# An attention and gated-MLP kernel: GpSimd's products and differences go to VectorE, and the first chunk's second product becomes native fp32

## The chip, the cores and the metric

The kernel runs on one core of one Trainium2 chip. The metric is device time in microseconds (us). Before the change three runs gave 677.52, 677.85 and 678.15 us, so the median is 677.85.

The core has a matrix engine (TensorE, PE), whose weight loads are listed apart (PEld), and four others: VectorE (DVE), ScalarE (ACT), GpSimd (POOL) and SyncE (SP), which here issues nearly all transfers. Each engine executes its own instructions in the order in which they were written, and waits on semaphores for the others.

## What is computed

Attention over 4 batches of 8 heads, 768 positions and 64 dimensions, followed by an MLP on the 3072 x 512 result. Cut to what matters:

```python
k_sum = k.reshape(B, H, nb, block, D).max(axis=3)      # block = 32, nb = 24
v_sum = v.reshape(B, H, nb, block, D).mean(axis=3)
scores_l = scale * q @ k.T        # kept where |i - j| < 16
scores_s = scale * q @ k_sum.T + log(32)
a = softmax(concat(scores_l, scores_s))
x = a @ concat(v, v_sum)          # heads side by side: 3072 x 512
h = x @ w_in                      # 512 x 2048
g = h * erf(softplus(h))
out = g @ w_out                   # 2048 x 512
```

The two weight matrices come as float64, the rest as float32.

## The kernel before

**Chunks and periods.** The 3072 tokens are worked on in 8 chunks of 384. The hidden dimension of 2048 is cut into 4 groups of 512, so that there are 32 periods (k = 0 to 31); period k belongs to chunk k // 4 and group k % 4. A period does the first product of its group (`mm1`, lines 499-511), reads it out of PSUM (`hout`: tanh on ScalarE, a copy on VectorE), applies ln and erf on ScalarE (`logs`, `erfs`), and runs the second product of the period before (`mm2`, lines 555-567), which accumulates over the four groups of a chunk in three PSUM banks. In between stands the attention of a quad, one pair of heads of a chunk, four to five periods ahead: `scores`, `softmax`, `transp`, `av`, `xsplit`. The four quads of the first chunk are done before period 0, interleaved with its `mm1`.

**Precision.** A float32 number is cut into a high and a low part in the format fp32r, and a product becomes three matmuls: high by high, high by low and low by high. `xsplit` makes the parts of x (xh, xl), `gsplit` those of g (gh, gl), `convert` those of the weights. Each weight unit is 128 x 2 x 512 numbers, 16 units in all, eight of w_in and eight of w_out, two for each group.

**Converting a weight unit** (lines 259-285) takes five instructions: three on VectorE (lines 266, 269, 272) assemble a float32 word out of the raw halves of a float64 by shifts and masks, ScalarE casts it into the high part (line 276), and GpSimd subtracts to get the low part (line 279). All 16 are converted once, between the first quads and period 3, so that within the first chunk every product uses parts.

**GpSimd's share.** Beside those 16 subtractions, GpSimd makes the product g = wt x h (line 543) in the first periods (`k < early`, which is 5), where ScalarE casts the high part of g and xsplit's high part, and VectorE makes the low part (line 550). From period 5 on all of `gsplit` and `xsplit` is VectorE's. GpSimd also copies the block summaries into the key window (line 371) and, for the first chunk, into the value window (line 355).

**Buffers.** Sixteen SBUF slots of one unit each (w0 to w15) hold the weights. A raw unit lands in its slot and the parts are written over it. Before that some slots hold the first chunk's keys, queries, probabilities and values (line 310). The last two, w14 and w15, serve as scratch for the float32 words (`homes`, line 248), so the last two units of w_out are loaded only in period 3 (line 666).

**The order of the work.** The operations are first collected with their reads and writes (class `Plan`, lines 45-159). `Plan.due` gives each operation a due time, counted back from the matmuls that need it; `Plan.order` then fills the engines one instruction at a time by estimated durations, taking the ready operation that is due first, and where an operation may run on two engines, the one that would end it first. TensorE's operations stay nearly in written order, with a window of 60 operations for the first 330. SP issues the transfers in planned order too: one that waits for a buffer holds up those behind it. In the gaps of the first stretch `busy` (line 595) writes filler matmuls on zeros.

Of the kernel before, what the change touches and what calls it, by code (L numbers as in the profile page):

```python
# [9 lines left out]
F32 = mybir.dt.float32  # L10
# [13 lines left out]
T = S // NTH  # L24
# [16 lines left out]
def f32(ap):  # L41
    return ap.bitcast(F32)
# [120 lines left out]
def block_attention_mlp(ctx: ExitStack, tc: tile.TileContext, q_t, k_nat, k_win, v_tok, v_nat, v_win, w_in, w_out, out):  # L163
# [61 lines left out]
    slot_of = {u: n for n, u in enumerate(units)}  # L225
    tiles, raws, whl = {}, {}, {}

    def slot(n, shape, dtype, name):
        return sb(shape, dtype, name, f"w{n}")

    def wname(u):
        n = slot_of[u]
        return [f"w{n}"] + ([f"w{n}a", f"w{n}b"] if n in (14, 15) else [])

    def load_w(u):
        kind, g, r = u

        def go():
            rw = raws[u] = slot(slot_of[u], [128, 2, 512, 2], U32, "rw")
# [5 lines left out]
        dma(1049, go, w=wname(u))  # L245


    homes = ["w14a", "w14b", "w15a", "w15b"]
    part_of = {}

    def temp(home):
        if home[0] == "t":
            return sb([128, 2, 512], F32, "a32", home)
        n = home[1:3]
        if n not in part_of:
            part_of[n] = slot(int(n), [128, 2, 2, 512], F32, "a32s")
        return part_of[n][:, "ab".index(home[3])]

    def convert(u, home):

        w, s = wname(u), {}

        def a():
            s["t"] = temp(home)
            s["a"], s["rw"] = s["t"].bitcast(U32), raws.pop(u)
            nc.vector.tensor_scalar(s["a"], s["rw"][..., 1], 3, 0x3FFFFFFF, op0=ALU.logical_shift_left, op1=ALU.bitwise_and)  # L266

        def b():
            nc.vector.scalar_tensor_tensor(s["a"], s["rw"][..., 0], 29, s["a"], op0=ALU.logical_shift_right, op1=ALU.bitwise_or)  # L269

        def c():
            nc.vector.scalar_tensor_tensor(s["a"], s["rw"][..., 1], 0xC0000000, s["a"], op0=ALU.bitwise_and, op1=ALU.bitwise_or)  # L272

        def high():
            whl[u] = slot(slot_of[u], [128, 2, 2, 512], F32R, "w")
            nc.scalar.copy(whl[u][:, 0], s["t"])  # L276

        def low(e):
            e.tensor_tensor(whl[u][:, 1], s["t"], f32(whl[u][:, 0]), op=ALU.subtract)  # L279
# [30 lines left out]
    V_SLOTS, K_SLOTS, Q_SLOT, P_SLOTS, W_SLOTS = (14, 15), (7, 8), 9, (10, 11), (12, 13)  # L310
# [188 lines left out]
    def mm1(k, f, ccs=range(4)):  # L499
        ch, g = divmod(k, NG)  # L500
        bank = hbank(k, f)

        def go(cc):
            if cc == 0:
                hs[k, f] = tiles[bank] = ps(bank, bank)
            w = whl["i", g, cc // 2][:, :, cc % 2, f * 128:(f + 1) * 128]
            for n, (m, x) in enumerate(((0, 0), (0, 1), (1, 0))):
                nc.tensor.matmul(hs[k, f][:, 0:T], lhsT=w[:, m], rhs=xt[ch, cc][x], start=(cc == 0 and n == 0), stop=(cc == 3 and n == 2))  # L508
        for cc in ccs:
            n = (ch * NP + cc) % NX  # L510
            pe(0.52, lambda cc=cc: go(cc), wname(("i", g, cc // 2)) + [f"xh{n}", f"xl{n}"], [bank])

    def hout(k, f):
# [24 lines left out]

    def gsplit(k, n, mult, cast, sub):
        s = (2 * k + n) % 3  # L540

        def mul(e):
            e.tensor_tensor(hc[k, n], wt.pop((k, n)), hc[k, n], op=ALU.mult)  # L543

        def high(e):
            gs[k, n] = [sb([128, 2, T], F32R, m, f"{m}{n}") for m in ("gh", "gl")]
            copy(e, gs[k, n][0], hc[k, n])

        def low(e):
            e.tensor_tensor(gs[k, n][1], hc.pop((k, n)), f32(gs[k, n][0]), op=ALU.subtract)  # L550
        on(mult, mul, [f"wt{s}"], [f"hc{s}"])
        on(cast, high, [f"hc{s}"], [f"gh{n}"])
        on(sub, low, [f"hc{s}", f"gh{n}"], [f"gl{n}"])

    def mm2(k, fs=range(G), ts=range(NT)):
        ch, g = divmod(k, NG)

        def go(i, t):
            if g == 0 and i == 0:
                os_[ch, t] = tiles[f"o{t}"] = ps("ops", f"o{t}")  # L560
            x, w = gs[k, i // 2], whl["o", g, i // 2][:, :, i % 2]
            for n, (m, y) in enumerate(((0, 0), (0, 1), (1, 0))):
                nc.tensor.matmul(os_[ch, t], lhsT=x[y][:, i % 2, t * 128:(t + 1) * 128], rhs=w[:, m],  # L563
                                 start=(g == 0 and i == 0 and n == 0), stop=(g == NG - 1 and i == G - 1 and n == 2))
# [62 lines left out]
    for names_, slots in ((["kf0", "kf1"], K_SLOTS[:1]), (["kf2", "kf3"], K_SLOTS[1:]), (["qf0", "qf1", "qf2", "qf3"], (Q_SLOT,)),
                          (["pr0", "pr1"], P_SLOTS[:1]), (["pr2", "pr3"], P_SLOTS[1:]), (["vwf0", "vwf1", "vwg0", "vwg1"], W_SLOTS[:1]),
                          (["vwf2", "vwf3", "vwg2", "vwg3"], W_SLOTS[1:]), (["vt0"], V_SLOTS[:1]), (["vt1"], V_SLOTS[1:])):
        for n in slots:  # L630
            for m in [f"w{n}"] + ([f"w{n}a", f"w{n}b"] if n in V_SLOTS else []):
                P.last[m] = [y for x in names_ for y in P.last[x]]
                P.readers[m] = [y for x in names_ for y in P.readers.get(x, [])]
# [92 lines left out]
    import json; json.dump([[o['n'],o['on'],o['start'],o['end'],o['due'],o['r'],o['w'],sorted(o['deps'])] for o in plan],open('/tmp/plan.json','w'),default=list)  # L726
# [47 lines left out]
```

## Time and profile before

| | |
|---|---|
| median of 3 runs | 677.85 us |
| profiled execution, its own time | 678.82 us |
| span of the profiled execution | 677.0 us |
| TensorE busy | 654.4 us (97%) |
| VectorE busy | 432.5 us (64%) |
| ScalarE busy | 475.1 us (70%) |
| GpSimd busy | 82.7 us (12%) |
| mean granted TensorE clock | 0.989 |
| moved by DMA | 64.52 MB |

Rows of the profile name a line, an engine, an operation, the tiles written and read, the shape, and how many. In tables by group there follow the busy time, the mean of one in ns, and the engine's idle time before them with what ended it. In a timeline the first two numbers are the start and the length in us; instructions that follow each other are merged, and the records of neighbours overlap by somewhat under 0.1 us. Matmuls are pipelined, so that the length of one matmul's record is longer than the distance to the next. A native fp32 matmul shows as two records.

### The profile page before, as it was taken

The page shows a single profiled execution, that of the slowest core. Times are in us where ns is not written, and L with a number is a line of the kernel's source. Part 1 is how long each engine was busy: PE and PEld are TensorE (multiplying, and loading weights), DVE is VectorE, ACT ScalarE, POOL GpSimd, SP SyncE. Part 2 cuts the span into 40 slices and gives each one's busy share as a digit, 9 for nine tenths or more (in the row PEclk, how much of TensorE's full clock was granted, in tenths as well). Part 3 has the DMA queues.
Part 4 walks back from the last instruction along what each step waited for, and adds up shares of the span by engine and source line. Part 5 has one row for each costly group of instructions (what it writes and reads, how often), then busy time and mean ns, then how long its engine had stood idle before and what let it go on. Part 6 is the DMA issues. An engine that isn't in the chain of part 4 may idle for free.

```text
span 677.0 us, 11588 instructions
## 1 busy us (share of the span) xinstructions
PE 654.4 (97%) x4646; PEld 567.9 (84%) x4653; DVE 432.5 (64%) x637; ACT 475.1 (70%) x869; POOL 82.7 (12%) x75
## 2 busy tenths in 40 slices
PE   9889689989999999999999999999999999999997
PEld 4667478879988889999888889999888899999996
DVE  4999999985565557665565558655655555534443
ACT  2659568978766887677667877677677876757662
POOL 2443764650000000000000000000000000000000
PEclk9999799989999999999999999999999999999999
DMA  9987515421112253202111254103111130001001
GB/s 322 307 309 239 204 63 165 142 84 66 56 57 56 87 167 123 76 17 91 56 56 56 66 187 125 58 23 103 57 56 56 56 103 23 1 0 48 1 0 47
DMA packets 29717, 64.52 MB, mean 95 GB/s; under 512 B 2976, under 2 KB 11872, under 8 KB 29664
## 3 DMA queue, kind: packets, MB, share of 16 engines
q1 hardware_dynamic: 29232, 63.39, 29.4%
q8 instruction: 37, 0.61, 0.4%
q10 hardware_dynamic: 432, 0.39, 0.2%
q14 instruction: 16, 0.13, 0.1%
HBM read 55.41 MB, written 6.29 MB: 91 GB/s over the span
## 4 chain that ended last, share of the span: by engine, by line
PE 81%; DVE 15%; issue 2%; DMA 1%; ACT 1%; POOL 0%; DVEq 0%; POOLq 0%
PE ops L563 36%; PE h L508 35%; PE px L473 3%; PE pa L406 3%; DVE a32s L266 3%; DVE a32s L269 3%; PE pa L456 2%; DVE a32s L272 2%; DVE pr L446 1%; PE idle L598 1%; DVE hc L524 1%; DMA rw<-w_out 1%; DVE a L272 1%; DVE mx L442 1%; DVE mx L429 1%
## 5 line engine op out<-in xcount | busy, mean ns | idle before, releaser
L508 PE MATMUL h<-xh,w 128*128 128x384 f32 x1008 | 272.8, 341 | 3.9 <-ACT wt L519 2.7
L563 PE MATMUL ops<-w,gh 128*128 128x512 f32 x768 | 247.7, 397 | 0.0
L508 PEld LDWEIGHTS h<-xh,w 128*128 128x128 f32 x1008 | 184.9, 189 | 7.5 <-ACT wt L519 4.4
L508 PE MATMUL h<-xl,w 128*128 128x384 f32 x504 | 170.9, 339 | 1.5 <-DVE xl L489 1.5
L563 PEld LDWEIGHTS ops<-w,gh 128*128 128x128 f32 x768 | 144.9, 189 | 32.5
L736 ACT ACT_TABLE_LOAD x127 | 162.9, 1283 | 2.3
L519 ACT ACTIVATE wt<-h 128x384 f32<-128x384 f32 x126 | 60.9, 491 | 138.8 <-PE h L508 100.6
L563 PE MATMUL ops<-w,gl 128*128 128x512 f32 x384 | 150.8, 393 | 1.9 <-DVE gl L550 1.9
L524 DVE COPY hc<-h 128x384 f32<-128x384 f32 x126 | 69.9, 555 | 119.2 <-PE h L508 86.7
L508 PEld LDWEIGHTS h<-xl,w 128*128 128x128 f32 x504 | 95.1, 189 | 3.4 <-DVE xl L489 2.1
L563 PEld LDWEIGHTS ops<-w,gl 128*128 128x128 f32 x384 | 72.6, 189 | 17.0 <-DVE gl L550 2.4
L434 ACT ACTIVATE pr<-pr,mx 128x120 f32<-128x120 f32 x168 | 64.1, 383 | 9.9 <-DVE mx L442 9.9
L543 DVE TENSOR_TENSOR hc<-wt,hc 128x768 f32<-128x768 f32 x56 | 51.7, 955 | 25.0 <-ACT wt L537 25.0
L550 DVE TENSOR_TENSOR gl<-hc,gh 128x768 fp32r<-128x768 f32 x64 | 62.7, 982 | 2.3 <-ACT gh L219 1.9
L371 POOL COPY kw<-ksum 128x144 f32<-128x144 f32 x28 | 10.3, 368 | 413.4 <-DMA kw<-k_win 411.3
L532 ACT ACTIVATE wt<-wt,half_b 128x768 f32<-128x768 f32 x64 | 59.9, 938 | 0.8
L537 ACT ACTIVATE wt<-wt 128x768 f32<-128x768 f32 x64 | 51.4, 840 | 0.4
L438 DVE TENSOR_SCALAR rs<-sm 128x6 f32<-128x6 f32 x32 | 5.4, 168 | 50.7 <-ACT pr L434 50.0
L219 DVE CAST gh<-hc 128x768 fp32r<-128x768 f32 x56 | 29.2, 554 | 13.3 <-PE ops L563 13.2
L279 POOL TENSOR_TENSOR w<-a32s,w 128x1024 fp32r<-128x1024 f32 x12 | 34.0, 2836 | 29.4 <-ACT w L276 28.2
L456 PE MATMUL pa<-ident,pr 128*120 128x128 f32 x168 | 23.7, 278 | 8.1 <-DVE pr L446 8.1
L434 ACT ACTIVATION_READ_ACCUMULATOR pr<-pr,mx 128x1 f32 x168 | 31.4, 187 | 0.0
(87 smaller groups left out, 564.6 us busy)
## 6 DMA issues: line engine op xcount, KB each, us to landing
kw<-k_win SPq DMA_DIRECT2D x28, 360.0 KB
rw<-w_in SPq DMA_DIRECT2D x8, 1024.0 KB
rw<-w_out SPq DMA_DIRECT2D x8, 1024.0 KB
vw<-v_win SPq DMA_DIRECT2D x28, 288.0 KB
qb<-q_t SPq DMA_DIRECT2D x28, 192.0 KB
out<-ob SPq DMA_DIRECT2D x21, 256.0 KB
kvn<-v_nat SPq DMA_DIRECT2D x12, 384.0 KB
kvn<-k_nat SPq DMA_DIRECT2D x12, 384.0 KB
```

The costliest lines, as they stand in the source:

```text
L279: e.tensor_tensor(whl[u][:, 1], s["t"], f32(whl[u][:, 0]), op=ALU.subtract)
L434: nc.scalar.activation(s["pr"][:, j], s["pr"][:, j], AF.Exp, scale=0.125, bias=s["mx"][:, j:j + 1], accum_out=sm[:, j:j + 1])
L456: nc.tensor.transpose(tp[0:NK, a, i * 128:(i + 1) * 128], s["pr"][:, NI * a + i], ident)
L508: nc.tensor.matmul(hs[k, f][:, 0:T], lhsT=w[:, m], rhs=xt[ch, cc][x], start=(cc == 0 and n == 0), stop=(cc == 3 and n == 2))
L519: nc.scalar.activation(wt[k, f // 2][:, f % 2], hs[k, f][:, 0:T], AF.Tanh, scale=0.5)
L524: nc.vector.tensor_copy(hc[k, f // 2][:, f % 2], hs[k, f][:, 0:T])
L532: act(0.86, lambda n=n: nc.scalar.activation(wt[k, n], wt[k, n], AF.Ln, scale=-0.49999994, bias=half_b), [s], [s], table="log")
L537: act(0.8, lambda n=n: nc.scalar.activation(wt[k, n], wt[k, n], AF.Erf, scale=-1.0), [s], [s], table="sig", after=after)
L543: e.tensor_tensor(hc[k, n], wt.pop((k, n)), hc[k, n], op=ALU.mult)
L550: e.tensor_tensor(gs[k, n][1], hc.pop((k, n)), f32(gs[k, n][0]), op=ALU.subtract)
L563: nc.tensor.matmul(os_[ch, t], lhsT=x[y][:, i % 2, t * 128:(t + 1) * 128], rhs=w[:, m], start=(g == 0 and i == 0 and n == 0), stop=(g == N ...
L736: nc.scalar.preload_act_table_set(sets[o["load"]])
```

## The change

- `convert` subtracts on VectorE instead of GpSimd, and does so for w_in only. A unit of w_out is only assembled into float32 (`w32`) in the first chunk.
- `mm2` in the first chunk (`ch == 0`) is one native fp32 matmul per pair of a group's slice and a token tile, with g whole and w_out whole, in place of three fp32r ones: 48 native ones for 144. `gsplit` there is only the product, on VectorE; no cast, no low part.
- `parts` is new: in periods 4 to 7 it makes the high part (ScalarE) and the low part (VectorE) of w_out, two units per period, ahead of the chunk's first `mm2`. For the last unit the low part is made in another buffer and copied.
- `gsplit`'s product is on VectorE in all periods. Up to period 4 the copies of h out of PSUM and xsplit's high part may each go to VectorE or ScalarE, as the plan finds.
- The slots are dealt out anew: raw units of w_in in w0 to w7, raw units of w_out in turn in w8 to w11, whole units of w_out in w12 to w14 and two half slots (a6, a7), which also serve as scratch for w_in. Six units instead of seven are loaded ahead, six more are written at period 0 and four at period 1, none at period 3.

```diff
-        on({"DVE": 0.69}, lambda e: a(), w, [home])
-        on({"DVE": 1.22}, lambda e: b(), w + [home], [home])
-        on({"DVE": 1.22}, lambda e: c(), w + [home], [home])
-        act(1.05, high, [home], w)
-        on({"POOL": 2.6}, low, [home], w)
+        on({"DVE": 0.69}, lambda e: a(), [w], [home] + ([f"a{m + 1}"] if u[0] == "o" and m in (0, 2, 4) else []))
+        on({"DVE": 1.22}, lambda e: b(), [w, home], [home])
+        on({"DVE": 1.22}, lambda e: c(), [w, home], [home])
+        if u[0] == "i":
+            act(1.05, high, [home], [w])
+            on({"DVE": 1.22}, low, [home], [w])
+
+    def parts(u):
+
+        m = number(u)
+        n, home = 8 + m, f"a{m}"
+        frees = [f"a{2 * (n - 12)}", f"a{2 * (n - 12) + 1}"] if 12 <= n < 15 else []
+        if m < 7:
+            def high():
+                t = slot(n, [128, 2, 2, 512], F32R, "w")
+                whl[u] = t[:, 0], t[:, 1]
+                nc.scalar.copy(whl[u][0], w32[u])
+
+            def low(e):
+                e.tensor_tensor(whl[u][1], w32.pop(u), f32(whl[u][0]), op=ALU.subtract)
+            act(1.05, high, [home], [f"w{n}"] + frees)
+            on({"DVE": 1.22}, low, [home, f"w{n}"], [f"w{n}"])
+            return
...
     def gsplit(k, n, mult, cast, sub):
         s = (2 * k + n) % 3
+        if k < NG:
+            def whole(e):
+                gs[k, n] = [sb([128, 2, T], F32, "gw", f"gh{n}")]
+                e.tensor_tensor(gs[k, n][0], wt.pop((k, n)), hc.pop((k, n)), op=ALU.mult)
+            on(mult, whole, [f"wt{s}", f"hc{s}"], [f"gh{n}"])
+            return
...
-            x, w = gs[k, i // 2], whl["o", g, i // 2][:, :, i % 2]
+            x, first, last = gs[k, i // 2], g == 0 and i == 0, g == NG - 1 and i == G - 1
+            if ch == 0:
+                nc.tensor.matmul(os_[ch, t], lhsT=x[0][:, i % 2, t * 128:(t + 1) * 128], rhs=w32["o", g, i // 2][:, i % 2], start=first, stop=last)
+                return
...
-    for u in units[7:14]:
-        load_w(u)
...
+    loads = {0: units[6:12], 1: units[12:16]}
+    early = 5
...
-        if k < early:
-            mult, cast, sub = {"POOL": 2.1}, {"ACT": 0.83}, {"DVE": 0.96}
-            xeng = {"ACT": 0.5}
-        else:
-            mult, cast, sub = {"DVE": 0.96}, {"DVE": 0.57}, {"DVE": 0.96}
-            xeng = {"DVE": 0.56}
+        mult = sub = {"DVE": 0.96}
+        cast = {"DVE": 0.57}
+        xeng, heng = ({"DVE": 0.56, "ACT": 0.5},) * 2 if k < early else ({"DVE": 0.56},) * 2
         if k == 3:
-            for u in units[14:16]:
-                load_w(u)
-            homes = ["t0", "t1"]
             turn(k)
             sums(k)
         for u in todo.get(k, []):
-            convert(u, homes[nconv % len(homes)])
-            nconv += 1
+            convert(u, f"a{6 + number(u) % 2}")
+        for u in loads.get(k, []):
+            load_w(u)
+        if NG <= k < 2 * NG:
+            for r in range(2):
+                parts(("o", k - NG, r))
```

More of the change, by code (lines that the diff above doesn't have):

```diff
@@ L224, in block_attention_mlp, with number, raw_slot @@
     units = [(kind, g, r) for kind, g in order for r in range(2)]
-    slot_of = {u: n for n, u in enumerate(units)}
-    tiles, raws, whl = {}, {}, {}
+    tiles, raws, whl, w32 = {}, {}, {}, {}
     def slot(n, shape, dtype, name):
         return sb(shape, dtype, name, f"w{n}")
-    def wname(u):
-        n = slot_of[u]
-        return [f"w{n}"] + ([f"w{n}a", f"w{n}b"] if n in (14, 15) else [])
+    def number(u):
+        return 2 * u[1] + u[2]
+    def raw_slot(u):
+        return number(u) if u[0] == "i" else 8 + number(u) % 4
     def load_w(u):
         kind, g, r = u
+        n = raw_slot(u)
         def go():
-            rw = raws[u] = slot(slot_of[u], [128, 2, 512, 2], U32, "rw")
+            rw = raws[u] = slot(n, [128, 2, 512, 2], U32, "rw")
             if kind == "i":
@@ L244, in go, with convert @@
             nc.sync.dma_start(out=rw, in_=src)
[L245 to L261, printed above, removed]
-        def a():
-            s["t"] = temp(home)
+        dma(1049, go, w=[f"w{n}"])
+    wide = {}
+    def convert(u, home=None):
+        w, s, m = f"w{raw_slot(u)}", {}, number(u)
+        if u[0] == "o":
+            home = f"a{m}"
+        def a():
+            if u[0] == "i" or m >= 6:
+                s["t"] = sb([128, 2, 512], F32, "a32", home)
+                if u[0] == "o":
+                    w32[u] = s["t"]
+            else:
+                if m % 2 == 0:
+                    wide[m // 2] = slot(12 + m // 2, [128, 2, 2, 512], F32, "a32s")
+                s["t"] = w32[u] = wide[m // 2][:, m % 2]
             s["a"], s["rw"] = s["t"].bitcast(U32), raws.pop(u)
@@ L274, in high, with low, move @@
         def high():
-            whl[u] = slot(slot_of[u], [128, 2, 2, 512], F32R, "w")
-            nc.scalar.copy(whl[u][:, 0], s["t"])
+            t = slot(raw_slot(u), [128, 2, 2, 512], F32R, "w")
+            whl[u] = t[:, 0], t[:, 1]
+            nc.scalar.copy(whl[u][0], s["t"])
         def low(e):
-            e.tensor_tensor(whl[u][:, 1], s["t"], f32(whl[u][:, 0]), op=ALU.subtract)
-        on({"DVE": 0.69}, lambda e: a(), w, [home])
-        on({"DVE": 1.22}, lambda e: b(), w + [home], [home])
-        on({"DVE": 1.22}, lambda e: c(), w + [home], [home])
-        act(1.05, high, [home], w)
-        on({"POOL": 2.6}, low, [home], w)
+            e.tensor_tensor(whl[u][1], s["t"], f32(whl[u][0]), op=ALU.subtract)
+        on({"DVE": 0.69}, lambda e: a(), [w], [home] + ([f"a{m + 1}"] if u[0] == "o" and m in (0, 2, 4) else []))
[11 more added lines that the diff above has]
+                t = slot(n, [128, 2, 2, 512], F32R, "w")
+                whl[u] = t[:, 0], t[:, 1]
+                nc.scalar.copy(whl[u][0], w32[u])
[4 more added lines that the diff above has]
+            return
+        def high():
+            whl[u] = [sb([128, 2, 512], F32R, "wh", "a6")]
+            nc.scalar.copy(whl[u][0], w32[u])
+        def low(e):
+            tiles["t1"] = sb([128, 2, 512], F32R, "wl", "t1")
+            e.tensor_tensor(tiles["t1"], w32.pop(u), f32(whl[u][0]), op=ALU.subtract)
+        def move(e):
+            whl[u].append(sb([128, 2, 512], F32R, "wl", "a7"))
+            copy(e, whl[u][1], tiles["t1"])
+        act(1.05, high, ["a7"], ["a6"])
+        on({"DVE": 1.22}, low, ["a6", "a7"], ["t1"])
+        on({"DVE": 0.75}, move, ["t1"], ["a7"])
     def load_nat(b, p):
@@ L505, in go, with hout @@
                 hs[k, f] = tiles[bank] = ps(bank, bank)
-            w = whl["i", g, cc // 2][:, :, cc % 2, f * 128:(f + 1) * 128]
+            w = [t[:, cc % 2, f * 128:(f + 1) * 128] for t in whl["i", g, cc // 2]]
             for n, (m, x) in enumerate(((0, 0), (0, 1), (1, 0))):
-                nc.tensor.matmul(hs[k, f][:, 0:T], lhsT=w[:, m], rhs=xt[ch, cc][x], start=(cc == 0 and n == 0), stop=(cc == 3 and n == 2))
+                nc.tensor.matmul(hs[k, f][:, 0:T], lhsT=w[m], rhs=xt[ch, cc][x], start=(cc == 0 and n == 0), stop=(cc == 3 and n == 2))
         for cc in ccs:
             n = (ch * NP + cc) % NX
-            pe(0.52, lambda cc=cc: go(cc), wname(("i", g, cc // 2)) + [f"xh{n}", f"xl{n}"], [bank])
-    def hout(k, f):
+            pe(0.52, lambda cc=cc: go(cc), [f"w{2 * g + cc // 2}", f"xh{n}", f"xl{n}"], [bank])
+    def hout(k, f, eng):
         bank, s = hbank(k, f), (2 * k + f // 2) % 3
@@ L519, in tanh, with hcopy @@
             nc.scalar.activation(wt[k, f // 2][:, f % 2], hs[k, f][:, 0:T], AF.Tanh, scale=0.5)
-        def hcopy():
+        def hcopy(e):
             if f % 2 == 0:
                 hc[k, f // 2] = sb([128, 2, T], F32, "hc", f"hc{s}")
-            nc.vector.tensor_copy(hc[k, f // 2][:, f % 2], hs[k, f][:, 0:T])
+            copy(e, hc[k, f // 2][:, f % 2], hs[k, f][:, 0:T])
         act(0.5, tanh, [bank], [f"wt{s}"], table="sig")
-        on({"DVE": 0.56}, lambda e: hcopy(), [bank], [f"hc{s}"])
+        on(eng, hcopy, [bank], [f"hc{s}"])
     def logs(k):
@@ L560, in go @@
                 os_[ch, t] = tiles[f"o{t}"] = ps("ops", f"o{t}")
-            x, w = gs[k, i // 2], whl["o", g, i // 2][:, :, i % 2]
+            x, first, last = gs[k, i // 2], g == 0 and i == 0, g == NG - 1 and i == G - 1
+            if ch == 0:
+                nc.tensor.matmul(os_[ch, t], lhsT=x[0][:, i % 2, t * 128:(t + 1) * 128], rhs=w32["o", g, i // 2][:, i % 2], start=first, stop=last)
+                return
+            w = [t[:, i % 2] for t in whl["o", g, i // 2]]
             for n, (m, y) in enumerate(((0, 0), (0, 1), (1, 0))):
-                nc.tensor.matmul(os_[ch, t], lhsT=x[y][:, i % 2, t * 128:(t + 1) * 128], rhs=w[:, m],
-                                 start=(g == 0 and i == 0 and n == 0), stop=(g == NG - 1 and i == G - 1 and n == 2))
+                nc.tensor.matmul(os_[ch, t], lhsT=x[y][:, i % 2, t * 128:(t + 1) * 128], rhs=w[m], start=first and n == 0, stop=last and n == 2)
         for i in fs:
             for t in ts:
-                pe(0.7, lambda i=i, t=t: go(i, t), wname(("o", g, i // 2)) + [f"gh{i // 2}", f"gl{i // 2}"], [f"o{t}"])
+                m = 2 * g + i // 2
+                if ch == 0:
+                    pe(0.87, lambda i=i, t=t: go(i, t), [f"a{m}", f"gh{i // 2}"], [f"o{t}"])
+                else:
+                    pe(0.7, lambda i=i, t=t: go(i, t), (["a6", "a7"] if m == 7 else [f"w{8 + m}"]) + [f"gh{i // 2}", f"gl{i // 2}"], [f"o{t}"])
     def evac(ch, t):
@@ L607, in block_attention_mlp @@
         load_vw_first(p)
-    for u in units[:7]:
+    for u in units[:6]:
         load_w(u)
@@ L625, in block_attention_mlp @@
             mm1(0, f, (p,))
[L627 to L633, printed above, removed]
-    for u in units[7:14]:
-        load_w(u)
+    for n, left in ((V_SLOTS[0], ["vt0"]), (V_SLOTS[1], ["vt1"]), (K_SLOTS[0], ["kf0", "kf1"]), (K_SLOTS[1], ["kf2", "kf3"]),
+                    (Q_SLOT, ["qf0", "qf1", "qf2", "qf3"]), (P_SLOTS[0], ["pr0", "pr1"]), (P_SLOTS[1], ["pr2", "pr3"]),
+                    (W_SLOTS[0], ["vwf0", "vwf1", "vwg0", "vwg1"]), (W_SLOTS[1], ["vwf2", "vwf3", "vwg2", "vwg3"])):
+        for m in [f"w{n}"] + ([f"a{2 * (n - 12)}", f"a{2 * (n - 12) + 1}"] if n >= 12 else []):
+            P.last[m] = [y for x in left for y in P.last[x]]
+            P.readers[m] = [y for x in left for y in P.readers.get(x, [])]
     load_quad(NP)
@@ L680, in block_attention_mlp @@
             mm1(k, 1)
-        hout(k, 1)
+        hout(k, 1, heng)
         if k != 3:
```

8 lines of the change are left out of this document (3 added, 5 removed).

## The prediction

> **What bounds the kernel now.** I read first the busy time of each engine by stretch, then the time-ordered chain of waits, then the timelines of VectorE (DVE), GpSimd (POOL) and TensorE (PE) where the stretches show loss. Rows of the stretches:
>
> ```profile
> core 0: us, PE busy (x) PEld busy (x) DVE busy (x) ACT busy (x) POOL busy (x), PEclk, DMA share, GB/s
> 17.60:51.00 33.40, 28.95 (x338) 20.94 (x340) 33.00 (x43) 18.95 (x57) 15.19 (x10) 1.00 0.96 310
> 51.00:62.70 11.70, 11.31 (x102) 10.36 (x104) 11.36 (x18) 10.56 (x17) 2.42 (x1) 1.00 0.59 211
> 62.70:91.30 28.60, 21.92 (x120) 14.32 (x120) 28.60 (x26) 20.33 (x42) 17.96 (x9) 0.82 0.62 209
> 91.30:113.60 22.30, 19.68 (x141) 17.10 (x140) 22.30 (x21) 13.92 (x24) 13.04 (x6) 1.00 0.25 71
> 113.60:134.10 20.50, 19.87 (x140) 17.12 (x139) 19.88 (x25) 19.74 (x39) 12.58 (x6) 1.00 0.52 177
> 134.10:158.40 24.30, 21.41 (x141) 18.94 (x140) 17.87 (x22) 19.69 (x35) 11.07 (x5) 0.93 0.24 72
> 177.50:196.70 19.20, 19.20 (x140) 17.22 (x139) 10.90 (x19) 13.63 (x25) 0.31 (x1) 1.00 0.17 50
> ```
>
> VectorE is busy throughout from 17.6 to 113.6 us and nearly so to 134; after 158.4 TensorE is full and VectorE has 8.3 of 19.2 us free. The four stretches that end at 91.3, 113.6, 134.1 and 158.4 each end with the last matmul of one period's second product: mm2(0) to mm2(3), the first chunk's. The chain of waits gives the rhythm that follows:
>
> ```profile
> 150.00 8.39 PE ops L563 x36
> 158.39 4.23 PE h L508 x24
> 169.22 8.60 PE ops L563 x36
> 590.27 8.39 PE ops L563 x36
> ```
>
> From 150.00 to 590.27 lie 23 periods, so one takes 19.14 us, of which the 36 matmuls of mm2 take 8.4, mm1 another 8.4 (two groups such as that at 158.39) and the attention the remaining 2.35. Nothing the change does after its second chunk alters that rhythm. So the question is when mm2(3) ends, now at 158.4. Against 19.14 the last three stretches lose 3.2, 1.4 and 5.2 us. The stretch from 62.7 holds only a quad's attention and mm2(0), 10.75 us of TensorE work, and takes 28.6: it loses 17.85.
>
> ```profile
> 62.78 4.91 PE L598 MATMUL idle<-zeros 128*128 128x512 bf16 x22
> 72.37 1.51 PE L456 MATMUL pa<-ident,pr 128*120 128x128 f32 x6 [4.67 <-DVE pr L446]
> 81.42 0.56 PE L563 MATMUL ops<-w,gl 128*128 128x512 f32 x1 [1.94 <-DVE gl L550]
> ```
>
> TensorE runs filler matmuls, waits for the probabilities of VectorE, then for the low part of the product (gl). Why VectorE is late there stands in the two timelines:
>
> ```profile
> 17.63 0.69 DVE L266 TENSOR_SCALAR a<-rw 128x1024 uint32<-128x1024 uint32 x1
> 18.35 1.22 DVE L269 SCALAR_TENSOR_TENSOR a<-rw,a 128x1024 uint32<-128x1024 uint32 x1
> 66.48 3.31 DVE L272 SCALAR_TENSOR_TENSOR a32s<-rw,a32s 128x1024 uint32<-128x1024 uint32 x1
> 69.72 2.50 DVE L446 TENSOR_TENSOR pr<-pr,rs 128x720 f32<-128x720 f32 x1
> 73.01 4.19 DVE L266 TENSOR_SCALAR a32s<-rw 128x1024 uint32<-128x1024 uint32 x2
> 77.12 3.38 DVE L269 SCALAR_TENSOR_TENSOR a32s<-rw,a32s 128x1024 uint32<-128x1024 uint32 x1
> ```
>
> ```profile
> 65.34 3.37 POOL L279 TENSOR_TENSOR w<-a32s,w 128x1024 fp32r<-128x1024 f32 x1 [1.17 <-DVE rs L438]
> 68.67 5.22 POOL L543 TENSOR_TENSOR hc<-wt,hc 128x768 f32<-128x768 f32 x2
> 73.85 5.57 POOL L279 TENSOR_TENSOR w<-a32s,w 128x1024 fp32r<-128x1024 f32 x2
> ```
>
> The same instructions take 0.69 and 1.22 us at 18 us, with no GpSimd arithmetic running; later one takes 3.3 and two take 4.2 while GpSimd multiplies or subtracts. The slow ones start inside GpSimd's spans, at low DMA load (71 GB/s from 91 us) as well as at high, so the transfers aren't their cause.
>
> **The change, part by part.**
>
> ```profile
> L279 POOL TENSOR_TENSOR w<-a32s,w 128x1024 fp32r<-128x1024 f32 x12 | 34.0, 2836 | 29.4 <-ACT w L276 28.2 <-DVE rs L438 1.2
> L279 POOL TENSOR_TENSOR w<-a,w 128x1024 fp32r<-128x1024 f32 x4 | 11.3, 2814 | 13.1 <-ACT w L276 12.6 <-POOL vwf L355 0.5
> L543 POOL TENSOR_TENSOR hc<-wt,hc 128x768 f32<-128x768 f32 x8 | 19.4, 2432 | 3.2 <-ACT wt L537 3.2
> L266 DVE TENSOR_SCALAR a32s<-rw 128x1024 uint32<-128x1024 uint32 x12 | 19.0, 1607 | 0.0
> L269 DVE SCALAR_TENSOR_TENSOR a32s<-rw,a32s 128x1024 uint32<-128x1024 uint32 x12 | 20.5, 1717 | 0.0
> L272 DVE SCALAR_TENSOR_TENSOR a32s<-rw,a32s 128x1024 uint32<-128x1024 uint32 x12 | 17.8, 1481 | 0.0
> L446 DVE TENSOR_TENSOR pr<-pr,rs 128x720 f32<-128x720 f32 x28 | 30.3, 1081 | 0.8
> L446 DVE TENSOR_TENSOR prf<-prf,rs 128x720 f32<-128x720 f32 x4 | 3.6, 904 | 0.0
> L550 DVE TENSOR_TENSOR gl<-hc,gh 128x768 fp32r<-128x768 f32 x64 | 62.7, 982 | 2.3 <-ACT gh L219 1.9
> L543 DVE TENSOR_TENSOR hc<-wt,hc 128x768 f32<-128x768 f32 x56 | 51.7, 955 | 25.0 <-ACT wt L537 25.0
> L276 ACT CAST w<-a32s 128x1024 fp32r<-128x1024 f32 x12 | 12.5, 1042 | 7.7 <-DVE a32s L272 7.7
> ```
>
> *GpSimd's 24 instructions go.* What VectorE gets back is its blocking: L266 12 x (1.61 - 0.69) = 11.0, L269 12 x (1.72 - 1.22) = 6.0, L272 12 x (1.48 - 1.22) = 3.1, L446 28 x (1.081 - 0.904) = 5.0, so 25 us from these groups; the smaller ones would add some. The GpSimd copies of k_win and v_win parts remain.
>
> The Trainium skill (SBUF — State Buffer, Who interferes with whom) calls the port pair of VectorE and GpSimd an exclusive lock held for a whole instruction. By it at most the 64.7 us of the three GpSimd groups could come back; the groups show some 25. If the rest were blocking too, the rival of the TensorE floor (below) would be the time.
>
> *What VectorE takes on in the first chunk.* Eight products of 0.96 (7.6) replace eight low parts gl of 0.98 (7.9): nothing. The eight differences of w_in, 128x1024, are not in the trace on VectorE; bounds are 1.18, below the 1.22 of the two-input L269 of that size, and 0.982 x 1024/768 = 1.31. I take 1.22: 9.8. So VectorE's work up to the end of the first chunk falls by 25 - 9.8 = 15 us. Copies of h out of PSUM and xsplit's may now go to ScalarE or VectorE; ScalarE loses the eight gh casts and eight w_out casts of 1.04 there and has 8 to 9 us free in two of the stretches. I count no gain for it, it is within the slack below.
>
> *The native product.* 12 whole-fp32 matmuls replace 36 fp32r ones per period of the first chunk. The trace has the kind once, in the summaries of v (L350), two records to a product:
>
> ```profile
> 8.27 1.02 PE L350 MATMUL vs<-vt,pick 128*120 128x512 f32 x2
> 12.80 3.69 PE L350 MATMUL vs<-vt,pick 128*120 128x512 f32 x8
> L350 PE MATMUL vs<-vt,pick 128*120 128x512 f32 x12 | 5.8, 608 | 0.0
> L350 PEld LDWEIGHTS vs<-vt,pick 128*120 128x120 f32 x12 | 2.0, 182 | 1.7 <-issue 1.5
> ```
>
> Eight records span 3.69 with the last one 0.61 long: (3.69 - 0.61)/7 = 0.44 apart, 0.88 to a product; the pair gives 1.02 - 0.61 = 0.41, so 0.82. Nothing overlapped would be 2 x 0.608 = 1.22. I take 0.87, nearest to the longer row: mm2 takes 12 x 0.87 = 10.4, 2.0 more than now, and a period of the first chunk 21.1.
>
> *When mm2(3) ends.* (a) The start of the second period's mm1, now at 51.0: VectorE has 33.0 of 33.4 us busy before it; the 25 us of blocking, shared out by GpSimd's busy time (15.2 there, 57.1 in the five stretches after), put 5 of them here; it gets two to four differences (2.4 to 4.9): -1.5, between -3 and +1. (b) The stretch from 62.7: the instructions at 66.48 and 69.72 lose 2.1 and 1.6 of blocking, so the probabilities come at about 67 rather than 72.2; the product no longer waits 5.2 for GpSimd, for ScalarE's cast and for gl. After the probabilities come 2.35 of attention, with one copy between, so mm2(0) starts at about 69.6 and ends at 80.0: 17.3 instead of 28.6, -11.3. The bounds are no idle at all (12.75) and a start at 75, where VectorE does all that it does now, only unblocked (the four rows from 66.48 hold 2.1 + 1.6 + 2.8 + 2.2 = 8.7 of blocking, less two differences, so 81.4 becomes 75). (c) The three stretches after it, 67.1 now, become 3 x 21.1 = 63.3 and some idle, since VectorE stays nearly as full as TensorE; I allow 2.0: -1.8 (bounds -3.8 and +1).
>
> *Loads.* Six units instead of seven are issued ahead, six in period 0 and four in period 1, on SP, in order with the quads' loads. The last w_out now arrives late, after its buffers served as scratch:
>
> ```profile
> 133.58 0.69 DVE L266 TENSOR_SCALAR a<-rw 128x1024 uint32<-128x1024 uint32 x1 [0.58 <-DMA rw<-w_out]
> ```
>
> After the change its loads wait only for the raw w_out two units earlier. I cost the move at nothing: the transfers use 0.25 to 0.62 of the DMA time from 62.7 on. If SP did wait there, the quads' loads queue behind it and the scores wait; two units at 310 GB/s are 6.8 us, which (b)'s and (c)'s upper bounds take in.
>
> *The parts of w_out, in the second chunk.* Eight casts of 1.04 on ScalarE (8.3), eight differences of 1.22 and one copy of about 0.6 on VectorE (10.4): 2.1 and 2.6 per period. The row 177.50 shows 5.6 us of ScalarE and 8.3 of VectorE free in such a period: that free time hides them, all but +0.6 for tanh instructions that queue behind a cast. Without that cover they cost 18.7.
>
> Sum: -1.5 - 11.3 - 1.8 + 0.6 = -14.0. The profiled execution's own time is 678.8 (span 677.0 and 1.8 around it), so 664.8; it lies 1.0 above the median of the runs, 677.85, on which the forecast is **663.9, say 664**.
>
> **The rivals.** *B, VectorE still sets the order*: mm2(0) starts at 75 and ends at 85.4 (-5.9), (c) comes out at +1, (a) at -0.5, the second chunk at +0.6: -4.8, 673. For it: VectorE's 100% up to 113.6. Against it: the product and the probabilities are due earlier than conversions, and the queue order is made by due time.
>
> *D, the TensorE floor*: all idle goes: the losses 17.85 + 3.2 + 1.4 + 5.2 = 27.7, less 4 x 2.0 for the native product, and (a) at -3: -22.7, 655. For it: smaller groups were blocked too, and the planned order will fit the real durations better. Against it: two engines that are nearly equally full wait for each other.
>
> *C, slower: the second chunk gives it back.* TensorE takes its matmuls in order there, so mm1 behind a late tanh, or mm2 behind a late part of w_out, stops everything. All 18.7 exposed: 677.85 - 14.6 + 18.7 = 682; it decides from 14.6 us, 3.7 per period of the 4.7 added. Against it are the 5.6 and 8.3 us free.
>
> *L, weight loads aren't hidden*: a native product costs 1.22, mm2 14.6, 4.2 more in each of four periods: 664 + 17 = 681. Against it are the rows 0.44 apart with 0.18 loads between. The Trainium skill (TensorE: Matmul & The Clock Gate, Part 3, The mechanism) says that a weight load overlaps a running matmul only when their row groups differ; the rows of L350, full-height products 0.44 apart, don't bear that out.
>
> *E, the change doesn't free VectorE*: the long durations have another cause. Then 9.8 us of differences are added to the bound engine: 688. The timelines speak against it.
>
> **How the numbers follow.** Forecast 0.60, B 0.18, D 0.12, C 0.05, L 0.03, E 0.02. What a measurement of this kernel can tell from no change is about 0.2%, 1.4 us. B's upper end reaches that with 0.03. So faster 0.60 + 0.15 + 0.12 = 0.87, same 0.03, slower 0.10. The range is 653 to 675: it takes in D and most of B, and leaves out C, L, E and the tails of B and D, about 0.17.
>
> **What would show it.** Right: L266, L269 and L272 at 0.7, 1.2 and 1.2 us; mm2(0) starting near 70; mm2(3) ending near 144; native records 0.44 apart; TensorE without gaps in the second chunk. Wrong: VectorE still 100% busy with TensorE idle before mm2(0) (B), gaps in front of mm1 or mm2 after 145 us (C), records 0.6 apart (L), long L266 with an idle GpSimd (E).

## The result, and the profile after

The changed kernel takes 661.76 us (median of 4 runs, 661.29 to 662.01) against 678.0 for the kernel before (one more run than in the median above); the ratio is 0.976, with a 95% interval of 0.9743 to 0.9777. That is 16.2 us less; 664 was forecast.

The stretches of the profiled execution after (span 660.0 us; PEclk is the granted share of TensorE's full clock), cut at the same events as those of before: the start of period 1's mm1 (48.9), its end (60.1), and the ends of mm2(0) to mm2(4).

```profile
core 0: us, PE busy (x) PEld busy (x) DVE busy (x) ACT busy (x) POOL busy (x), PEclk, DMA share, GB/s
0.00:48.90 48.90, 46.18 (x490) 29.29 (x490) 38.54 (x62) 24.41 (x77) 8.88 (x25) 1.00 0.96 313
48.90:60.10 11.20, 11.18 (x103) 10.46 (x104) 10.45 (x16) 11.11 (x25) 0.00 (x0) 1.00 1.02 369
60.10:76.60 16.50, 16.50 (x97) 8.31 (x95) 16.35 (x24) 14.23 (x28) 1.52 (x2) 1.00 0.88 297
76.60:98.00 21.40, 21.40 (x130) 15.08 (x129) 19.34 (x23) 15.32 (x28) 0.08 (x1) 1.00 0.50 164
98.00:119.30 21.30, 21.30 (x129) 15.04 (x128) 20.16 (x28) 20.21 (x38) 2.11 (x2) 1.00 0.33 101
119.30:140.60 21.30, 21.30 (x129) 15.05 (x128) 16.57 (x22) 19.39 (x36) 0.31 (x1) 1.00 0.21 63
140.60:160.00 19.40, 19.40 (x141) 17.26 (x140) 14.05 (x22) 16.68 (x30) 0.76 (x1) 1.00 0.27 91
```

The stretch that ends with mm2(0) took 28.6 us and takes 16.5. There VectorE is still full (16.35 of 16.5 us), and TensorE spends some 4 us on fillers. The three stretches after it took 67.1 and take 64.0, and in each of them TensorE is busy to the last tenth, although VectorE still works 78 to 95% of the time. So from mm2(0) on the two engines have changed places: VectorE was full and TensorE waited, now TensorE is full.

The waits before had a second price. Behind them TensorE's granted clock was lower for a while: PEclk was 0.82 in the stretch of 28.6 us and 0.93 in that of 24.3, and it is 1.00 in every stretch after. Two rows of before show it. Behind the wait that ended at 72.37, six fillers take 2.77 us, where 22 had taken 4.91 ahead of it; behind the wait that ended at 141.46, 24 matmuls of mm1 take 6.01 us, where 24 take 4.23 at 158.39.

```profile
73.67 2.77 PE L598 MATMUL idle<-zeros 128*128 128x512 bf16 x6
142.36 6.01 PE h L508 x24
```

An estimate from the two clocks is 0.18 x 28.6 + 0.07 x 24.3 = 6.8 us at most, some of it while TensorE waited again anyway. So a part of the 17.0 us by which the spans differ is not waiting itself but slow matmuls behind the waits; no run separates the two.

The chain of waits says the same. VectorE made 15% of it and makes 1%; DMA made 1% and makes 5%. First its shares before, then those after with some of its pieces:

```profile
PE 81%; DVE 15%; issue 2%; DMA 1%; ACT 1%; POOL 0%; DVEq 0%; POOLq 0%
PE 92%; DMA 5%; DVE 1%; ACT 1%; SPq 0%; issue 0%
...
7.58 12.45 DMA vwf<-v_win
20.04 15.78 DMA rw<-w_in
...
87.52 10.50 PE ops L605 x24
108.83 10.50 PE ops L605 x24
130.13 10.50 PE ops L605 x24
151.47 8.59 PE ops L609 x36
640.00 16.50 PE ops L609 x72
```

The native second product (L605) takes 10.50 us for 24 records, two to a product, so 0.875 to each of the 12 products. From 7.6 to 35.8 us the chain hangs on transfers: the fill now follows the loading (313 GB/s and a DMA share of 0.96 up to 48.9 us).

The groups of VectorE's conversions after, to be read against 1607, 1717 and 1481 ns before:

```profile
L268 DVE TENSOR_SCALAR a<-rw 128x1024 uint32<-128x1024 uint32 x10 | 7.0, 699 | 1.0 <-DMA rw<-w_in 1.0
L271 DVE SCALAR_TENSOR_TENSOR a<-rw,a 128x1024 uint32<-128x1024 uint32 x10 | 12.8, 1276 | 0.0
L274 DVE SCALAR_TENSOR_TENSOR a<-rw,a 128x1024 uint32<-128x1024 uint32 x10 | 12.1, 1214 | 0.0
L482 DVE TENSOR_TENSOR pr<-pr,rs 128x720 f32<-128x720 f32 x28 | 25.4, 907 | 0.8
L282 DVE TENSOR_TENSOR w<-a,w 128x1024 fp32r<-128x1024 f32 x8 | 9.7, 1218 | 0.2
```

### The profile page after: what moved, and what is told of

Same layout as the page of the kernel before. It is cut to its first block, busy times and chain, and to the rows that moved or that the text cites. A ratio compares the mean times of both kernels' runs of the same rounds, so it can differ in the third digit from the quotient of the medians.

```text
span 660.0 us, 11458 instructions
## 1 busy us (share of the span) xinstructions
PE 653.7 (99%) x4600; PEld 554.5 (84%) x4600; DVE 414.9 (63%) x644; ACT 473.1 (72%) x871; POOL 19.8 (3%) x51
## 4 chain that ended last, share of the span: by engine, by line
PE 92%; DMA 5%; DVE 1%; ACT 1%; SPq 0%; issue 0%
PE h L544 40%; PE ops L609 36%; PE ops L605 6%; PE px L509 4%; PE pa L442 3%; PE pa L492 3%; DMA rw<-w_in 2%; DMA vwf<-v_win 2%; DMA kf<-k_nat 1%; PE idle L647 1%; DVE a L271 0%; ACT pr L470 0%; PE px L341 0%; ACT L780 0%; DVE a L274 0%; DVE w L282 0%
## 5 line engine op out<-in xcount | busy, mean ns | idle before, releaser
L609 PE MATMUL ops<-w,gh 128*128 128x512 f32 x588 | 189.5, 396 | 0.0
L219 DVE COPY hc<-h 128x384 f32<-128x384 f32 x117 | 65.2, 557 | 122.7 <-PE h L544 86.6
L609 PEld LDWEIGHTS ops<-w,gh 128*128 128x128 f32 x588 | 110.4, 188 | 25.0
L609 PE MATMUL ops<-w,gl 128*128 128x512 f32 x294 | 115.0, 391 | 0.0
L609 PEld LDWEIGHTS ops<-w,gl 128*128 128x128 f32 x294 | 55.2, 188 | 11.1
L568 ACT ACTIVATE wt<-wt,half_b 128x768 f32<-128x768 f32 x64 | 60.1, 938 | 0.8
L592 DVE TENSOR_TENSOR gl<-hc,gh 128x768 fp32r<-128x768 f32 x56 | 53.1, 952 | 0.4
L605 PE MATMUL ops<-a32s,gw 128*128 128x512 f32 x72 | 31.9, 596 | 0.0
L457 DVE TENSOR_TENSOR pr<-pa,mask_sb 128x720 f32<-128x720 f32 x28 | 25.4, 906 | 5.2 <-PE pa L442 5.2
```

The source lines that it names most:

```text
L219: e.copy(o, i) if e is nc.scalar else e.tensor_copy(o, i)
L568: act(0.86, lambda n=n: nc.scalar.activation(wt[k, n], wt[k, n], AF.Ln, scale=-0.49999994, bias=half_b), [s], [s], table="log")
L605: nc.tensor.matmul(os_[ch, t], lhsT=x[0][:, i % 2, t * 128:(t + 1) * 128], rhs=w32["o", g, i // 2][:, i % 2], start=first, stop=last)
```

## The experiments

The theory is that GpSimd's arithmetic held up VectorE, which set the pace of the first chunk, and that the native product costs TensorE 2 us per period but, with less work on VectorE, leaves it the only full engine. The first rival is that no instruction was held up and the gain is only the work that left the first chunk.

### One part of the change alone

In the kernel before, only GpSimd's work goes to VectorE:

```diff
-        on({"POOL": 2.6}, low, [home], w)
+        on({"DVE": 1.22}, low, [home], w)
...
-            mult, cast, sub = {"POOL": 2.1}, {"ACT": 0.83}, {"DVE": 0.96}
+            mult, cast, sub = {"DVE": 0.96}, {"ACT": 0.83}, {"DVE": 0.96}
```

> The kernel before with one part of the change: all 16 weight differences and the eight early products go from GpSimd to VectorE; the second product stays in three fp32r matmuls and everything else as before. VectorE gets 16 x 1.22 + 8 x 0.96 = 27 us of work in the first chunk and loses its blocking (25 us from the larger groups, somewhat more with the smaller). Theory blocking: the two cancel, 670 to 682 us. Rival work (GpSimd's work was free help and the durations had another cause): 27 us on the bound engine, 695 or more.

Measured: 671.56 us against 677.57 for the kernel before, run beside it (ratio 0.9912, 0.9888 to 0.9937): 6.0 us less, with 27 us more work on VectorE. The rival is out. The rows from mm1(1) to the end of mm2(3):

```profile
50.00:78.00 28.00, 26.57 (x210) 20.25 (x211) 26.51 (x35) 25.82 (x44) 1.18 (x2) 1.00 0.78 272
78.00:99.60 21.60, 19.90 (x140) 16.84 (x138) 19.90 (x26) 17.73 (x28) 0.00 (x0) 1.00 0.24 62
99.60:126.50 26.90, 23.13 (x141) 19.39 (x140) 25.77 (x35) 20.10 (x41) 1.12 (x2) 0.87 0.42 136
126.50:150.40 23.90, 21.19 (x141) 18.43 (x140) 22.19 (x32) 21.62 (x41) 0.45 (x1) 0.93 0.30 97
```

The groups of the conversions are back at 0.69 to 0.70 and 1.21 to 1.36 us, yet VectorE is busy 92 to 96% of each stretch and TensorE is idle for 1.7 to 3.8 us in each of the last three. Behind those waits the clock falls again: at 0.87 and 0.93 TensorE needs 23.1 and 21.2 busy us for a period that takes 19.3 later. The work itself is too much for VectorE as long as all parts are made in the first chunk.

Next comes the other part, nearly alone: the changed kernel with GpSimd back at its old work on w_in and on the first chunk's products, some 42 of its 65 us. The differences of w_out stay on VectorE, in the second chunk. In this kernel and in the one with only the products on GpSimd, `w32` is also looked up without removing the entry.

```diff
-            on({"DVE": 1.22}, low, [home], [w])
+            on({"POOL": 2.6}, low, [home], [w])
...
-        mult = sub = {"DVE": 0.96}
+        sub = {"DVE": 0.96}
+        mult = {"POOL": 2.1} if k < early else {"DVE": 0.96}
```

> The changed kernel with GpSimd back at its old work in the first chunk: the eight w_in differences and the products of periods 0 to 3; native second product and late parts of w_out stay. GpSimd is then busy some 42 us of the 65 taken away. Theory blocking: 42/65 of 25 to 34 us come back as blocking, less 17 us of work that leaves VectorE, and the products come 1.5 us later on the way to the second product: 664 to 672. Rival work: VectorE has 17 us less to do, so 655 to 660, the floor of TensorE.

Measured: 677.2 us, ratio 0.9989 (0.998 to 0.9998): as good as no gain, 5 us above what the theory allowed and far from the rival. VectorE has 17 us less to do than in the changed kernel and is full again in the stretches of mm2(0) and mm2(1):

```profile
62.00:85.20 23.20, 20.49 (x108) 10.43 (x108) 23.20 (x24) 15.13 (x33) 11.42 (x6) 0.93 0.85 281
85.20:113.70 28.50, 24.41 (x130) 17.86 (x128) 28.25 (x28) 18.68 (x32) 14.56 (x6) 0.88 0.40 133
113.70:135.00 21.30, 21.30 (x129) 15.05 (x128) 18.20 (x22) 18.56 (x33) 4.18 (x3) 1.00 0.28 82
```

The clocks of 0.93 and 0.88 in the first two rows are an estimated 0.07 x 23.2 + 0.12 x 28.5 = 5.0 us at most, which the expectation had no term for.

So the parts are worth 6.0 and 0.4 us alone and 16.2 together. Each alone leaves VectorE full in places, by work in the one case and by blocking in the other.

### GpSimd's two jobs apart

Each of the two edits of the last diff alone.

> The changed kernel with only the eight w_in differences on GpSimd (2.8 us each, 22 us). Theory blocking: 9 to 12 us of blocking for 9.8 us of work saved on VectorE: 660 to 665. Rival work: 655 to 660.

> The changed kernel with only the early products on GpSimd (2.4 us each for 0.96). Theory blocking: 7 to 10 us of blocking for 7.6 us of work saved, and each second product waits 1.5 to 3 us longer for its operand: 663 to 672. Rival work: 656 to 661.

Measured: with only the w_in differences on GpSimd 672.01 us (ratio 0.9915, 0.9898 to 0.9931), 7 us above the expected span; with only the products 667.47 (0.9849, 0.9834 to 0.9864), inside it. Against 661.76 these are +10.2 and +5.7, together 15.9, near the +15.4 of the run with both.

Why 9.8 us less work on VectorE made the kernel 10.2 slower is seen in its timelines between 45 and 73 us, VectorE first, GpSimd second:

```profile
45.91 2.74 DVE L268 TENSOR_SCALAR a32s<-rw 128x1024 uint32<-128x1024 uint32 x1
64.39 3.35 DVE L274 SCALAR_TENSOR_TENSOR a<-rw,a 128x1024 uint32<-128x1024 uint32 x1
69.41 3.96 DVE L580 TENSOR_TENSOR gw<-wt,hc 128x768 f32<-128x768 f32 x2
```

```profile
45.71 2.39 POOL L282 TENSOR_TENSOR w<-a,w 128x1024 fp32r<-128x1024 f32 x1
64.28 2.38 POOL L282 TENSOR_TENSOR w<-a,w 128x1024 fp32r<-128x1024 f32 x1 [0.99 <-ACT w L279]
68.90 2.79 POOL L282 TENSOR_TENSOR w<-a,w 128x1024 fp32r<-128x1024 f32 x1 [2.24 <-ACT w L279]
```

Three differences hold up three steps, by 2.0, 2.1 and 2.1 us over the unblocked 0.69, 1.22 and 2 x 0.95, and the last two lie on the way to mm2(0): the probabilities and the product itself. mm2(0) ends at 86.9 instead of 76.8. Of these 10.1 us the three account for 6.2 by their lengths and the clock for 2.0: TensorE waited until 72.56 for the product, and from there to 77.17, at half clock for most of it, it takes 4.6 us for what took 2.6. The rest isn't traced; steps of VectorE are also longer earlier, one of 0.17 us takes 1.99 at 23.74. The periods after mm2(0) are full on TensorE (its rows from 86.7 on show 21.4 of 21.4, 21.3 of 21.3 and 21.3 of 21.3 us). So what is saved on VectorE after mm2(0) is worth nothing there, and what is lost before it counts. The expectation had set the blocking off against the saved work as if both counted alike.

### GpSimd work that nobody waits for

The kernels above also change which engine makes which operand. These two only add GpSimd work on a scratch tile, behind five copies of the first chunk:

```diff
...
             e.tensor_copy(s["kw"][:, :, LW:NK], ksum[:, p:p + 1, :].to_broadcast([128, NB, NS]))
+            for _ in range(12 if NP < qd <= NP + 5 else 0):
+                e.tensor_tensor(scr, scr, scr, op=ALU.mult)
...
```

and in the other `range(30 ...)` with `e.memset(scr, 0.0)`.

> The changed kernel with work added that nobody waits for: behind each of five GpSimd copies of the first chunk, twelve products of a scratch tile (128x256, two inputs) with itself, some 40 us of GpSimd in all. Same instructions and order on all other engines. Theory blocking: VectorE's two-input instructions (a 1.22 us group of the conversions) grow to 1.3 to 1.8 on the mean, and with VectorE nearly full the time becomes 667 to 680. Rival (durations had another cause, such as the data flow between the engines): lengths unchanged, 661 to 663.

> As the run with added products, but with thirty fills of the scratch tile behind each copy, which write and read nothing. If any GpSimd instruction blocks VectorE: as there, 667 to 680. If only reads meet VectorE's second input: the two-input instructions keep 1.22 us, the one-input shift and mask (0.69) may still grow, and the time is 661 to 666.

Measured: with products 667.97 us (ratio 0.9844, 0.9825 to 0.9863), 6.2 above the changed kernel; with fills 662.33 (0.9761, 0.9745 to 0.9778), as the changed kernel. The groups with products, then with fills:

```profile
L412 POOL TENSOR_TENSOR scr<-scr 128x256 f32<-128x256 f32 x60 | 67.8, 1131 | 4.3
L273 DVE SCALAR_TENSOR_TENSOR a<-rw,a 128x1024 uint32<-128x1024 uint32 x10 | 14.0, 1397 | 0.0
L276 DVE SCALAR_TENSOR_TENSOR a<-rw,a 128x1024 uint32<-128x1024 uint32 x10 | 13.2, 1322 | 0.0
L270 DVE TENSOR_SCALAR a<-rw 128x1024 uint32<-128x1024 uint32 x10 | 8.5, 849 | 1.0 <-DMA rw<-w_in 1.0
```

```profile
L412 POOL MEMSET scr<- 128x256 f32 x150 | 49.7, 332 | 8.3
L273 DVE SCALAR_TENSOR_TENSOR a<-rw,a 128x1024 uint32<-128x1024 uint32 x10 | 12.8, 1276 | 0.0
L276 DVE SCALAR_TENSOR_TENSOR a<-rw,a 128x1024 uint32<-128x1024 uint32 x10 | 12.1, 1214 | 0.0
L270 DVE TENSOR_SCALAR a<-rw 128x1024 uint32<-128x1024 uint32 x10 | 7.1, 723 | 0.0
```

No VectorE instruction reads or writes what the products work on, yet they lengthen VectorE's conversions by 0.11 to 0.15 us on the mean, and VectorE's busy time grows from 414.9 to 427.8 us. Fills leave the two-input ones at the 1276 and 1214 ns of the changed kernel. The added work isn't quite without a follower: weight loads of the scores are recorded as waiting 1.4 us for products. But they wait 1.5 us for fills too, and there the time stays. So the blocking is shown for GpSimd products and not seen for fills. Whether it is the reading that makes the difference is not shown by these two runs alone, since products and fills also differ in length (1131 and 332 ns on the mean). The Trainium skill (SBUF — State Buffer, Who interferes with whom) says that a VectorE instruction with two SBUF inputs contends with a GpSimd instruction that reads SBUF, not with one that only writes it; for the two-input conversions both runs agree (1397 and 1322 ns with products, 1276 and 1214 with fills). Of the one-input step that sentence says nothing: it takes 849 ns with products and 723 with fills, for 699.

### How full VectorE and TensorE are

The last step of each conversion is done twice, which gives the same value:

```diff
-            nc.vector.scalar_tensor_tensor(s["a"], s["rw"][..., 1], 0xC0000000, ...)
+            for _ in range(2):
+                nc.vector.scalar_tensor_tensor(s["a"], s["rw"][..., 1], 0xC0000000, ...)
```

> The changed kernel with the last step of each weight's conversion done twice on VectorE (same value): 16 x 1.14 = 18.2 us more VectorE work in the first chunk, none elsewhere. If VectorE and TensorE are nearly equally full there: 672 to 680. If TensorE alone sets the time and VectorE has room: 661.5 to 666.

Measured: 676.21 us (673.31 to 676.57; ratio 0.9954, 0.9932 to 0.9977). Of the 18.2 us added to VectorE 14.4 came out in the median (11.5 in the profiled execution). The five executions fall into two groups, 673.3 and 673.5 at a mean clock of 1.000 and 676.2 to 676.6 at 0.992 to 0.995, so some 3 us of the median go with the clock. VectorE is full at once in the stretches that end with mm2(0), mm2(1) and mm2(2):

```profile
52.00:82.20 30.20, 28.03 (x198) 18.59 (x200) 30.06 (x39) 23.39 (x46) 1.32 (x2) 1.00 0.77 267
82.20:105.00 22.80, 21.47 (x128) 14.83 (x126) 22.66 (x26) 16.11 (x26) 0.00 (x0) 1.00 0.46 151
105.00:130.60 25.60, 21.86 (x129) 15.07 (x129) 25.50 (x34) 21.05 (x45) 2.20 (x2) 1.00 0.32 99
```

So the changed kernel stands near the balance of the two engines.

### The parts in the second chunk

The cast and the difference of seven units are each done twice in `parts`:

```diff
-                nc.scalar.copy(whl[u][0], w32[u])
+                for _ in range(2):
+                    nc.scalar.copy(whl[u][0], w32[u])
```

and the difference likewise.

> The changed kernel with the casts and differences of seven of the eight w_out units of the second chunk done twice (same values): 7.3 us more on ScalarE and 8.5 on VectorE in periods 4 to 7. Forecast (hidden by free time): 661.5 to 664. Rival C (exposed): up to 677.

Measured: 670.29 us (ratio 0.9881, 0.9866 to 0.9895), 8.5 above the changed kernel: neither hidden nor all exposed. Where the parts lie in the changed kernel is the reason. Its differences of the parts (L303) by stretch, with VectorE's busy time on them, clock, DMA share and GB/s, and their row by tile:

```profile
119.30:140.60 21.30, 7.15 (x6) 1.00 0.21 63
140.60:160.00 19.40, 1.22 (x1) 1.00 0.27 91
160.00:179.10 19.10, 0.00 (x0) 1.00 0.17 50
...
L303 DVE TENSOR_TENSOR w<-a32s,w x6: 1218/1220/1226, 126.3 to 137.5; 128x1024 fp32r<-128x1024 f32 x6
```

The plan takes them early: six of the seven in one period, where that leaves ScalarE 1.9 us free and VectorE 4.7, and the cover of four periods isn't used. A second kernel keeps the doubled work but holds each period's two units back until that period's first mm1 group:

```diff
+            held = [len(P.ops) - 1]
+            for r in range(2):
+                parts(("o", k - NG, r), held)
...
-            act(1.05, high, [home], [f"w{n}"] + frees)
+            act(1.05, high, [home], [f"w{n}"] + frees, after=held)
```

> As the run with the parts done twice, but the two units of each of the periods 4 to 7 are held back in the plan until the first group of mm1 of that period, so that the doubled work spreads over four periods instead of crowding into the fourth and fifth. If the place of the parts cost the 8.5 us of the doubled run: 661.5 to 664.5. If their amount did: 668 or more.

> The changed kernel unaltered, beside the next run on the same chip: 661 to 662.5.

Measured: 664.97 us (ratio 0.981, 0.9796 to 0.9824); the changed kernel, run beside it, 661.98 (0.9766, 0.9753 to 0.9778). The cost of the doubled parts falls from 8.5 to 3.0 us, half a microsecond above what "place" allowed. Most of it was the place; the rest stays open (TensorE's one recorded wait from 119 to 165 us there is 2.1 us for a copy of h on VectorE).

### A version that is faster than both

If TensorE sets the time of the first chunk's last period, giving that period its fp32r parts back should pay. The slots of the parts are dealt out anew, and one unit is moved by two copies.

```diff
-            if ch == 0:
+            if k < NG - 1:
                 nc.tensor.matmul(...)
...
-        if NG <= k < 2 * NG:
+        for g_ in {NG: (NG - 1, 0), NG + 1: (1,), NG + 2: (2,)}.get(k, ()):
             for r in range(2):
-                parts(("o", k - NG, r))
+                parts(("o", g_, r))
```

> The changed kernel with the native second product for three groups of the first chunk only: the fourth uses fp32r parts, made at the start of period 4 (slots of the parts dealt out anew, one unit moved by two copies). TensorE loses 10.5 - 8.4 = 2.1 us, VectorE gets four casts and differences of the product (3.0 us) and earlier parts. If TensorE sets the time from the first second product on: 659.5 to 660.5. If VectorE does: 662 or more.

> The kernel with fp32r parts in the last group of the first chunk once more. If TensorE sets the time there, 1.3 to 2.1 us below the changed kernel in the same call; if the first difference was one between chips, equal to it.

Measured: 660.19 us (ratio 0.9733, 0.9718 to 0.9748) and, beside the changed kernel at 661.98, 659.77 (0.9736, 0.9722 to 0.975). These last two intervals don't meet: 2.2 us less, 0.1 more than expected. The stretch that ends with mm2(3) in that run:

```profile
119.60:138.80 19.20, 19.20 (x140) 17.21 (x139) 16.92 (x24) 17.70 (x33) 0.31 (x1) 1.00 0.24 71
```

19.2 us for 21.3, TensorE full, and VectorE with room for the additional work.

## Why the prediction was right

**The bound.** VectorE held up by GpSimd was a reason for TensorE's waits: the runs with GpSimd's old arithmetic and the one with added products show it. It wasn't the only one, since with GpSimd's arithmetic gone and all parts still made in the first chunk, VectorE's work alone kept the time at 671.56. Cases E and the native product with exposed weight loads (L) are out: conversions at 0.70 and 1.21 to 1.28 us, and 10.50 us for 24 native records, 0.44 to a record.

**The sum, term by term**, between the two profiled executions:

| step | forecast | measured |
|---|---|---|
| (a) start of mm1(1), 51.0 | -1.5 | -2.1 (48.9) |
| mm1(1) itself, 11.7 | 0 | -0.5 (11.2) |
| (b) stretch to the end of mm2(0), 28.6 | -11.3 | -12.1 (16.5) |
| (c) next three stretches, 67.1 | -1.8 | -3.1 (64.0) |
| rest of the kernel, 518.6 | +0.6 | +0.8 (519.4) |
| sum | -14.0 | -17.0 |

The spans differ by 17.0, the medians of the runs by 16.2. Up to the end of mm2(3) the forecast was -14.6 and -17.8 came out: it ended at 140.6 rather than near 144. The largest error of size is in (c): 2.0 us of idle were allowed because the engines are nearly equally full, and there is none; the three stretches are 64.0 for 63.3 of calculated TensorE work, and the 0.7 is the native period, 21.3 instead of 21.1. The run with doubled conversion steps shows how near that was.

**Not in the working: the clock.** The rows with PEclk 0.82 and 0.93 stand in the prediction, but it counted the whole loss of those stretches alike and gave the clock no term. The forecast for (b) and (c) came close without one, because it was built from undisturbed lengths and the clock stayed at 1.00 when the long waits were gone. That was an assumption left unsaid: several runs in which waits remained show 0.87 to 0.93 in a stretch.

**The native product** was priced at 10.4 per period and takes 10.50.

**The differences on VectorE** were priced at 1.22 and take 1.218.

**Wrong in its reason: the parts of w_out.** The working named the free time of four periods as the cover and +0.6 as the price. The rest of the kernel did come out 0.8 us longer, but the cover isn't as described: the plan puts nearly all parts into period 4, and at double the amount 8.5 of 15.8 us came out. That the price was so near owes something to luck.

**Loads** were costed at nothing from 62.7 us on, and TensorE has no wait there. Ahead of that they now lead the chain, which the working didn't say. That loading limits (a) is the chain's reading; no run varied it.

**The rivals.** B (673) would need VectorE to keep setting the order, and D (655) all idle gone; the result lies between the forecast and D. Of D's terms the idle did go in (c); what it assumed for (a), -3, and for (b), 12.75 us, did not come, since VectorE is full up to mm2(0) and TensorE still runs fillers while the probabilities are made. The timeline of the changed kernel:

```profile
59.94 3.84 PE L647 MATMUL idle<-zeros 128*128 128x512 bf16 x17
63.62 0.82 PE L492 MATMUL pa<-ident,pr 128*120 128x128 f32 x6
```

C didn't come, but its mechanism exists, as the doubled parts show.

## What to carry to other kernels

An engine that "helps" can take back more than it gives: compare the length of the same instruction where the helper is idle and where it works, before counting the help. Two changes that each leave the bound engine full by another cause are worth little alone and much together, so a part tested alone can be rejected wrongly. And work that is called hidden should be looked up in the trace after: a planner may put it all into the one period that has least room. Last, a wait of the matrix engine can cost more than its length: look at the granted clock of the stretch behind it.

## What the runs showed of the hardware

- GpSimd products of 128x256 on a scratch tile that nobody reads cost a kernel 6.2 us; 150 fills of the same tile, 49.7 us of GpSimd, cost nothing that can be measured (662.33 against 661.76, and 661.98 for the changed kernel measured again).
- A GpSimd difference of 2.4 us lengthened the VectorE instruction that met it by about 2.1 us (3.35 for 1.22, 2.74 for 0.69): nearly its whole length, and so one small step on VectorE waits for one large one on GpSimd. Taken over all of GpSimd's work the price is lower: some 25 us in the larger groups for 64.7 us of arithmetic.
- A native fp32 product of 128x128 by 128x512 takes 0.875 us in a row of them, against 0.70 for three fp32r matmuls (8.4 us for 36). Here, with GpSimd's arithmetic gone, the dearer product and the later parts were the cheaper by 9.8 us (661.76 against 671.56), since VectorE prepares less.
- Behind waits of 4.7 and 2.8 us for VectorE's probabilities TensorE went on at a lower granted clock: in the kernel before, 0.50 from 72 to 78 us and around 145, with fillers of some 0.46 us where they had taken 0.22.
